# Reordering the split temporaries, the weight sums and the first stores in the seven-product units of an attention-and-mixer kernel

## The chip, the cores and the metric

The kernel runs on one core of one Trainium2 chip. The metric is the device time of one execution in microseconds. Five engines matter here: PE (TensorE: matmul, with its weight loads, PEld, shown apart), DVE (VectorE), ACT (ScalarE), POOL (GpSimd), and SP (SyncE), whose queue issues nearly all DMAs. Each engine works through its own queue in the order in which the program gives it instructions; engines wait for one another through semaphores.

## The reference

The kernel computes two things in a row. The first is a decayed linear attention over blocks of 64 rows; its output x has 4 batches of 768 x 512. The second is a mixer over it, and this is where the change lies:

```python
xt = x.transpose(0, 2, 1)
h = np.maximum(xt @ w_tok1, 0.0) @ w_tok2          # token mixing, 768 -> 256 -> 768
u = x + h.transpose(0, 2, 1)
h2 = np.maximum(u @ w_ch1, 0.0) @ w_ch2            # channel mixing, 512 -> 1536 -> 512
return (u + h2).astype(np.float32)
```

All is in float32. A matrix product is made of three matmuls of halved operands: each operand is split into a high part (a rounded copy, made by ACT) and a low part (source minus high part, made by POOL or DVE), and the products high-high, low-high and high-low are summed in PSUM.

## The kernel before

**Units.** Channel mixing is cut into 24 units. A unit is one pair (g, b): a group g of 256 of the 1536 hidden channels (six groups, 0 to 5) for a batch b. Units 0 to 11 run through the groups upwards for batches 0 and 1; units 12 to 23 run through them downwards for batches 2 and 3, with units 21 and 22 swapped, so 21 is (0, 2) and 22 is (1, 3). The names in the code: `NP1` = 12, `FIRST` = 14, `NU` = 24.

**Seven products in place of eight.** Both matrix products of a unit are done on blocks of 2 x 2 with seven block products in place of eight. The first, u @ w_ch1, takes the hidden products m1 to m7 (six matmuls of 128 x 384 each). Its operands are blocks of u and differences of blocks (B11, B21, B22, T1 to T4), and combinations of weight blocks.

In most units the second product, hidden @ w_ch2, takes plain blocks: four pairs (`out_pair`, twelve matmuls each). In the units of `SEVEN`, which are 14 to 20 and 22, it too takes seven products, M1 to M7 (`out_seven`, six matmuls each). For these the unit has to make from its hidden blocks h11, h12, h21 and h22 the differences T1 to T4, each with a high and a low part, and from the weights w_ch2 the same combinations, here called weight sums (`sum_steps`). A unit's second product is always worked through one unit later: while m1 to m7 of unit n run on PE, the pairs or M1 to M7 of unit n-1 run between them.

**What sets the order.** All is written out by hand: the engines take their instructions in the order of the program. `SLOTS_OF` (L1106) lists for each kind of unit the order of hidden products (m), output products (M) or pairs (numbers 0 to 3), and of the step t. `background(n)` lists work put between the slots, each with the place from which it may go: a product counts 6 places and a pair 12 (`T_M`, `T_P`), a step such as t none, and after each slot all work whose place has been reached is issued.

**The steps of a seven-product unit** (`mixing_seven`, L866):

- m1: ACT copies the bank to scratch a (L890). m2: DVE adds (L895), ACT takes the relu (L896): this is h11, and its parts are made (`parts_of`: cast on ACT, L884; subtraction on POOL, L885).
- m6: builds on m1's bank; ACT copies it to scratch b (L901). m5: a copy to scratch c (L906). m7: builds on m1's bank, DVE adds (L910), relu (L911): h22 in c, and its parts. m3: builds on m5's bank, DVE adds (L916), relu (L917): h12 in b.
- t: a = b - a is T1 (L920), and its parts; b = c - b is T3 (L922); c = c - a is T2 (L923), and its parts.
- m4: builds on m1's bank; ACT takes the relu to scratch d (L928): h21. Then the parts of h21 and those of T3.
- The fourth difference, d - c (L934), and its parts are put behind m1 of the next unit (`fourth`).

The parts of T1 to T4 lie in one tile, `late_t`.

**Output products.** M1, M6, M7 and M4 use one PSUM pair, `pa` of L980, and M5, M3 and M2 another, `pc`; there are two pairs of banks in all. Behind each product DVE adds the pair to the result in `uT` (L986; for the plain pairs L1021), and a later product on the same pair waits for that addition. M5 is the first to use its pair, so it waits for the addition that last read those banks in the unit before: M4's, or that of the last plain pair.

**Weight sums.** `load_sums(g)` (L946) loads the saved w_ch2 group from DRAM by one DMA into a raw tile; `sum_steps(g)` gives eight steps: two splits (cast on ACT, L374; subtraction on POOL, L375), four DVE combinations (L548 to L551), and two more splits. They must be done before the output products of group g start.

**Stores.** A finished quarter of a batch is turned by two DVE transposes (L1040) into one of two buffers, `hh0` and `hl0`, in turn, and goes out by eight DMAs on SP (L1046). There are eight such stores for batches 0 and 1, called store 0 to 7 here. The raw weight groups from the second on use the buffer `hh0` too; the first (group 4) takes batch 0's `uT0`. SP also issues the loads that bring back saved weights (`restore`, L1093).

Of the kernel before, what the change touches and what calls it, by code (L numbers as in the profile page):

```python
# [22 lines left out]
def kernel(  # L23
# [171 lines left out]
    n = 1  # L195
# [201 lines left out]
    def words(b):  # L397
        return uT[b].rearrange("p t s -> p (t s)").bitcast(U32)
# [245 lines left out]
    for i in range(-2, NI):  # L644
# [26 lines left out]
        n = early.get(i, len(work) // 4)  # L671
# [28 lines left out]
        if i == 5:  # L700
            weights[0] = group_tiles(0, False)
            w, w3 = words(2), words(3)
# [12 lines left out]
        if i == 10:  # L715
            homes[0] = {"B11": (up, None, 1), "B21": (up, None, 1), "T2": (kp, "kn", 2), "T1": (kp, "qn", 2)}
            homes[0] |= {"B22": (kp, "kr", 2), "T3": (kp, "kT", 2), "T4": (kp, "qT", 2)}
            first = build(0, 0, on_vector=("T1", "T2", "T3", "T4", "B22"))
# [38 lines left out]
    steps = {}  # L757
# [15 lines left out]
    NP1 = NG * 2  # L773
    FIRST = NP1 + 2
    units = [(g, b) for g in range(NG) for b in (0, 1)] + [(g, b) for g in reversed(range(NG)) for b in (2, 3)]
    units[-3], units[-2] = units[-2], units[-3]
    NU = len(units)
    SEVEN = [n for n in range(FIRST, NU - 1) if units[n][0] > 0]
    hs = {}
    scratch, fourth = {}, {}  # L780
    late = {}

    def take_scratch():
# [83 lines left out]
    def mixing_seven(n):  # L867

        key = units[n]
        hs[n] = {}  # L870
        at = {}
        a, b, c, d = (scratch[x] for x in (f"a{n % 2}", f"b{n % 2}", "c", "d"))
        vec = nc.vector

        def parts_of(o, src):
            if o[0] == "T":
                if "T" not in late:
                    late["T"] = upool.tile([P, 8, SB], F32R, tag="uT0", name="late_t")
                k = 2 * int(o[1]) - 2
                hh, hl = late["T"][:, k], late["T"][:, k + 1]  # L880
            else:
                hh, hl = (cp.tile([P, SB], F32R, tag=f"h{o}{x}" + "0" * (o != "11"), name=f"h{o}{x}{n}") for x in "hl")
            hs[n][o] = hh, hl
            nc.scalar.copy(out=hh, in_=src)  # L884
            nc.gpsimd.tensor_sub(out=hl, in0=src, in1=hh.bitcast(F32))  # L885

        def m1():
            at["a"] = bank("xT" if n % 2 else "sh", f"pa{n}", SB)
            prod(key, at["a"], A11, "B11", True)
            nc.scalar.copy(out=a, in_=at["a"])  # L890

        def m2():
            at["b"] = bank("sh", f"pb{n}", SB)
            prod(key, at["b"], A12, "B21", True)
            vec.tensor_add(out=a, in0=at["b"], in1=a)  # L895
            nc.scalar.activation(a, a, AF.Relu)  # L896
            parts_of("11", a)

        def m6():
            prod(key, at["a"], S2, "T2", False)  # L900
            nc.scalar.copy(out=b, in_=at["a"])  # L901

        def m5():
            at["c"] = bank("sh", f"pc{n}", SB)
            prod(key, at["c"], S1, "T1", True)
            nc.scalar.copy(out=c, in_=at["c"])  # L906

        def m7():
            prod(key, at["a"], S3, "T3", False)
            vec.tensor_add(out=c, in0=at["a"], in1=c)  # L910
            nc.scalar.activation(c, c, AF.Relu)  # L911
            parts_of("22", c)

        def m3():
            prod(key, at["c"], S4, "B22", False)
            vec.tensor_add(out=b, in0=at["c"], in1=b)  # L916
            nc.scalar.activation(b, b, AF.Relu)  # L917

        def t():
            vec.tensor_sub(out=a, in0=b, in1=a)  # L920
            parts_of("T1", a)
            vec.tensor_sub(out=b, in0=c, in1=b)  # L922
            vec.tensor_sub(out=c, in0=c, in1=a)  # L923
            parts_of("T2", c)

        def m4():
            prod(key, at["a"], A22, "T4", False)
            nc.scalar.activation(d, at["a"], AF.Relu)  # L928
            parts_of("21", d)
            parts_of("T3", b)  # L930

        def u():
            e = cp.tile([P, SB], F32, tag="h12h0", name=f"t4_{n}")
            vec.tensor_sub(out=e, in0=d, in1=c)  # L934
            parts_of("T4", e)

        fourth[n] = u

        return {"m1": m1, "m2": m2, "m3": m3, "m4": m4, "m5": m5, "m6": m6, "m7": m7, "t": t}

    sums_of = {}

    def load_sums(g):
        pool, tag = (upool, "uT0") if g == NG - 2 else (hidp, "hh0")
        late["raw", g] = pool.tile([P, JG * DM], U32, tag=tag, name=f"sums_raw{g}")
        nc.sync.dma_start(out=sum_raw(g), in_=saved_c2[g])  # L946

    def sum_raw(g):
        return late["raw", g]

    def sum_steps(g):
        low = c2_tile(f"s{g}", g % 2).rearrange("p a t j -> p (a t j)")[:, 0 : NW * 2 * P]
        low = low.rearrange("p (m t j) -> p m t j", t=2, j=P)
        if g % 2:
            if "odd" not in late:
                late["odd"] = upool.tile([P, NW, 2, P], F32R, tag="uT1", name="sums_odd")
            high = [late["odd"][:, x] for x in range(NW)]
        else:
            h0, h1 = (cp.tile([P, 4, 2, P], F32R, tag=f"cs{x}", name=f"sums{g}{x}") for x in range(2))
            high = [(h0, h1)[x // 4][:, x % 4] for x in range(NW)]  # L960
        sums_of[g] = high, low
        v = [x.bitcast(F32).rearrange("p (m t j) -> p m t j", t=2, m=2) for x in (sum_raw(g)[:, 0:DM], sum_raw(g)[:, DM:])]
        if g % 2:
            return split_seven(high[A11], low[:, A11], [late["odd"][:, x : x + 2] for x in (0, 2, 4)], low, v, nc.vector)
        return split_seven(high[A11], low[:, A11], [h0[:, 0:2], h0[:, 2:4], h1[:, 0:2]], low, v, nc.vector)
# [61 lines left out]
    def store(b, x, between=None):  # L1027

        sh, t = x // 2, 2 * (x % 2)
        k = 2 * b + sh  # L1030
        y = ytags[0]
        ytags.rotate(-1)
        if isinstance(y, str):
            y = hidp.tile([P, 1024], F32, tag=y, name=f"y{k}{t}")
        y = y[:, : 2 * SB]
        y = y.rearrange("p (blk t q) -> p blk t q", t=2, q=32)
        ub = uT[b][:, t : t + 2, sh * SB : (sh + 1) * SB]
        to = out[b, sh * SB : (sh + 1) * SB].rearrange("(blk s) (t q c) -> q s blk t c", s=32, t=4, q=4)
        for tt in (t, t + 1):
            nc.vector.transpose(out=y[:, :, tt - t, :], in_=ub[:, tt - t])  # L1040
            if between and tt == t:
                between()
        for m in range(4):
            for tt in (t, t + 1):
                eng = nc.scalar if k == LAST - 1 and tt == 3 and m >= 2 else nc.sync
                eng.dma_start(out=to[m, :, :, tt], in_=y[m * 32 : (m + 1) * 32, :, tt - t])  # L1046
# [48 lines left out]
    def temp_tiles():  # L1095
# [9 lines left out]

    SLOTS_OF = {  # L1106
        (False, False): ("m1", "m6", 0, 1, "m2", "m7", "m5", 2, "m4", 3, "m3"),
        (True, False): ("m1", 0, 1, "m2", "m6", "m5", 2, "m7", "m3", "t", 3, "m4"),
        (True, True): "m1 M1 m2 M5 m6 M6 m5 M3 m7 M7 m3 M2 t m4 M4".split(),
        (False, True): "m1 M1 m6 M5 m2 M6 m7 M3 m5 M7 m4 M2 m3 M4".split(),  # L1110
    }

    def background(n):

        g, b = units[n]
        ev = []

        def add(when, *fs):
            ev.extend((when, f) for f in fs)
# [82 lines left out]
        if n == NP1 + 1:  # L1202
# [1 line left out]
            add(6, bl["T4.h"])  # L1204
            add(12, bl["T4.l"])
            add(36, bl["B22"])
        if n == NP1:
            add(84, lambda: store(0, 0))
            add(90, lambda: store(0, 1))
        if n == NP1 + 1:  # L1210
            add(36, lambda: store(0, 2))
            add(60, lambda: store(0, 3), lambda: load_sums(g - 1))
        if n == FIRST:
            add(24, lambda: store(1, 0))
            add(66, lambda: store(1, 1))
        if n == FIRST + 1:
            add(12, lambda: store(1, 2))
            add(48, lambda: store(1, 3))
        if FIRST < n < NU - 4 and n % 2:
            add(72, lambda: load_sums(g - 1))  # L1220
        if n in SEVEN and n % 2 == 0 and g not in sums_of:
            ss = sum_steps(g)
            add(12, ss[0], ss[1])
            add(48, *ss[2:7])
            add(60, ss[7])
        if n >= NU - 2:
            x = 2 * (n - NU + 2)
            add(36, lambda: store(2, x))
            add(84, lambda: store(2, x + 1))
# [9 lines left out]
    def run(n, slots):  # L1239
        ev, at, ms = background(n), 0, (mixing_seven if n in SEVEN else mixing)(n)  # L1240
        if n - 1 in SEVEN:
            ms |= out_seven(n - 1)
            ms["m1"] = lambda first=ms["m1"]: [first(), fourth[n - 1]()]
        for x in slots:
            if isinstance(x, str):
                ms[x]()
                at += T_M if len(x) > 1 else 0
            else:
                out_pair(x[0], x[1])
                at += T_P  # L1250
            while ev and ev[0][0] <= at:
                ev.popleft()[1]()
        while ev:
            ev.popleft()[1]()
# [53 lines left out]
```

## Time and profile before

| | |
|---|---|
| median of 3 runs | 569.49 us (569.33 to 569.65) |
| profiled execution | 569.2 us, of which the span 567.3 us |
| granted PE clock in it | 0.995 |
| PE, PEld busy | 545.4 us (96%), 528.2 us (93%) |
| DVE, ACT, POOL busy | 445.8 us (79%), 244.2 us (43%), 276.6 us (49%) |
| moved by DMA | 65.72 MB, a mean of 116 GB/s |

The span runs from the first to the last instruction of the program; some 1.9 us of the execution's time lie around it. In the rows, times are from the start of the span. A timeline row gives start, duration, engine, line of the kernel, operation, what is written and read, shape and count, and in brackets the engine's idle time before it and who ended it. A row of waits gives who waited for whom, the total in us, how many times, and the longest. Matmuls overlap: the next starts before the one before has ended.

### The profile page before, as it was taken

The page shows a single profiled execution, that of the slowest core. Times are in us where ns is not written, and L with a number is a line of the kernel's source. Part 1 is how long each engine was busy: PE and PEld are TensorE (multiplying, and loading weights), DVE is VectorE, ACT ScalarE, POOL GpSimd, SP SyncE. Part 2 cuts the span into 40 slices and gives each one's busy share as a digit, 9 for nine tenths or more (in the row PEclk, how much of TensorE's full clock was granted, in tenths as well). Part 3 has the DMA queues.
Part 4 walks back from the last instruction along what each step waited for, and adds up shares of the span by engine and source line. Part 5 has one row for each costly group of instructions (what it writes and reads, how often), then busy time and mean ns, then how long its engine had stood idle before and what let it go on. Part 6 is the DMA issues. An engine that isn't in the chain of part 4 may idle for free.

```text
span 567.3 us, 10786 instructions
## 1 busy us (share of the span) xinstructions
PE 545.4 (96%) x4186; PEld 528.2 (93%) x4186; DVE 445.8 (79%) x650; ACT 244.2 (43%) x490; POOL 276.6 (49%) x248
## 2 busy tenths in 40 slices
PE   5998999999999999999999999999989999999994
PEld 4887898999999999999999999999989999999994
DVE  4788887787786989788778787797588878886783
ACT  3465432435263454443434444444344455442421
POOL 6666642737214563534444444643456767572330
PEclk9999999999999999999999999999999999999998
DMA  9999999998003523442617200005846131320237
GB/s 185 256 230 199 180 180 195 197 170 150 1 3 112 200 80 130 143 153 74 242 39 241 75 0 1 1 3 87 213 69 188 55 113 56 112 75 1 34 58 133
DMA packets 176020, 65.72 MB, mean 116 GB/s; under 512 B 163553, under 2 KB 166753, under 8 KB 175969
## 3 DMA queue, kind: packets, MB, share of 16 engines
q1 hardware_dynamic: 172224, 63.75, 47.6%
q10 hardware_dynamic: 3744, 1.28, 0.9%
q8 instruction: 33, 0.54, 0.4%
q14 instruction: 19, 0.15, 0.1%
HBM read 48.24 MB, written 16.78 MB: 115 GB/s over the span
## 4 chain that ended last, share of the span: by engine, by line
PE 77%; DVE 11%; DMA 5%; ACT 2%; SPq 2%; issue 2%; ACTq 0%; DVEq 0%
PE po L1006 21%; PE pa L795 9%; PE pc L795 8%; PE pb L795 6%; PE ph L451 6%; PE pa L980 4%; PE pc L980 4%; PE pd L795 3%; PE pu L488 3%; PE xT L323 2%; PE sc L299 2%; DMA qn<-in_q_dram 2%; PE xT L333 2%; PE pu L471 1%; DMA c1lr<-dc1l 1%
## 5 line engine op out<-in xcount | busy, mean ns | idle before, releaser
L1021 DVE TENSOR_TENSOR uT<-po,uT 128x768 f32<-128x768 f32 x62 | 59.0, 953 | 23.8 <-PE po L1006 23.6
L286 POOL COPY stb<-sv 64x320 f32<-64x320 f32 x32 | 26.8, 839 | 43.4 <-DVE sv L273 42.5
L806 ACT ACTIVATE c<-c 128x384 f32<-128x384 f32 x42 | 22.1, 526 | 59.6 <-DVE c L851 32.5
L340 ACT COPY uT<-xT 128x384 f32<-128x384 f32 x32 | 15.3, 477 | 48.5 <-PE xT L333 48.5
L323 PE MATMUL xT<-a,vn 128*64 128x128 f32 x384 | 35.5, 277 | 0.0
L986 DVE TENSOR_TENSOR uT<-pa,uT 128x768 f32<-128x768 f32 x32 | 30.4, 948 | 5.6 <-PE pa L980 5.6
L808 POOL TENSOR_TENSOR h22l<-c,h22h 128x384 fp32r<-128x384 f32 x14 | 14.4, 1029 | 40.1 <-ACT h22h L807 40.1
L307 DVE TENSOR_TENSOR a<-sc,mask 128x768 f32<-128x768 f32 x32 | 29.1, 949 | 5.9 <-PE sc L299 5.7
L333 PE MATMUL xT<-qs,stb 128*64 128x128 f32 x320 | 31.1, 273 | 0.0
L375 POOL TENSOR_TENSOR c1l<-cs,c1h 128x512 fp32r<-128x512 f32 x15 | 19.2, 1292 | 23.2 <-ACT c1h L374 23.2
L986 DVE TENSOR_TENSOR uT<-pc,uT 128x768 f32<-128x768 f32 x24 | 22.8, 949 | 9.3 <-PE pc L980 9.3
L451 PE MATMUL ph<-xhi,w1h 128*128 128x256 f32 x96 | 28.2, 294 | 0.8 <-DVE uT L493 0.5
L1006 PE MATMUL po<-h12h,c 128*128 128x384 f32 x112 | 28.7, 337 | 0.0
L1006 PE MATMUL po<-h11h,c 128*128 128x384 f32 x112 | 28.6, 336 | 0.0
L1006 PE MATMUL po<-h22h,c 128*128 128x384 f32 x112 | 28.6, 336 | 0.0
L1006 PE MATMUL po<-h21h,c 128*128 128x384 f32 x112 | 28.6, 336 | 0.0
L451 PE MATMUL ph<-xhi,w1l 128*128 128x256 f32 x96 | 27.1, 282 | 0.0
L451 PE MATMUL ph<-xlo,w1h 128*128 128x256 f32 x96 | 27.1, 282 | 0.0
L299 PE MATMUL sc<-qT,kT 64*128 64x128 f32 x384 | 26.0, 282 | 0.2 <-ACT qT L237 0.2
L299 PEld LDWEIGHTS sc<-qT,kT 64*128 64x128 f32 x384 | 22.9, 189 | 3.3 <-issue 1.8
L252 POOL TENSOR_TENSOR qs<-qT,lamp 128x640 f32<-128x640 f32 x16 | 25.3, 1583 | 0.3
L364 DVE TENSOR_TENSOR xlo<-xp,xhi 128x384 fp32r<-128x384 f32 x32 | 17.7, 552 | 9.1 <-ACT xhi L363 8.8
(402 smaller groups left out, 1947.5 us busy)
## 6 DMA issues: line engine op xcount, KB each, us to landing
raw<-in_moe_w_ch_dram SPq DMA_DIRECT2D x20, 512.0 KB, 3.8
vn<-in_v_dram SPq DMA_DIRECT2D x16, 384.0 KB, 5.3
kn<-in_k_dram SPq DMA_DIRECT2D x30, 192.0 KB, 5.0
out_dram<-y SPq DMA_DIRECT2D x96, 48.0 KB, 1.9
qn<-in_q_dram SPq DMA_DIRECT2D x44, 96.0 KB, 3.4
kr<-in_k_dram SPq DMA_DIRECT2D x32, 96.0 KB, 3.4
dc1h<-c1h SPq DMA_DIRECT2D x4, 768.0 KB, 5.3
dc1l<-c1l SPq DMA_DIRECT2D x4, 768.0 KB, 6.7
```

What stands on the lines that cost most here:

```text
L252: nc.gpsimd.tensor_mul(out=qss[i], in0=qTs[i][:, P:].rearrange("p (c i) -> p c i", i=P), in1=lamp[:, p, None, :].broadcast_to([P, NC - 1, P]),
L286: nc.gpsimd.tensor_copy(out=st[r, :, h, :], in_=sv[r].rearrange("p (e c) -> p c e", c=NC - 1))
L299: nc.tensor.matmul(out=sc[h][:, c * P : (c + 1) * P], lhsT=kTs[i][r, cs], rhs=qTs[i][r, cs], start=True, stop=True,)
L307: nc.vector.tensor_mul(out=a, in0=pair.rearrange("p h (c i) -> p h c i", i=P), in1=mask[:, 2 * p : 2 * p + 2, None, :].broadcast_to([P, 2, ...
L323: nc.tensor.matmul(out=xT[h * D : (h + 1) * D, cs], lhsT=vns[i][:, h, c, :], rhs=weights_of[i, g, h][:, cg, :], start=(cg == 0), stop=False,)
L333: nc.tensor.matmul(out=xT[h * D : (h + 1) * D, cs], lhsT=st[:, c - 1, h, :], rhs=qss[i][:, c - 1, :], start=False, stop=(cg == 2),)
L451: nc.tensor.matmul(out=ph, lhsT=w[:, c, fs], rhs=x[:, c], start=(i == 0), stop=(i == 3 * NC - 1))
L795: nc.tensor.matmul(out=to, lhsT=w[:, t], rhs=x[:, t], start=(start and i == 0), stop=(i == 5), skip_group_check=not start,)
L980: nc.tensor.matmul(out=pair[x][:, t], lhsT=w[:, t], rhs=h, start=(start and i == 0), stop=(i == 2), skip_group_check=not start,)
L986: nc.vector.tensor_add(out=ub, in0=pair[x], in1=ub)
L1006: nc.tensor.matmul(out=to, lhsT=w[:, jj, t * P : (t + 1) * P], rhs=h, start=(i == 0), stop=(i == 3 * JG - 1))
L1021: nc.vector.tensor_add(out=ub, in0=po, in1=ub)
```

## The change

No operation on data is added or removed; five things are moved.

- The subtraction that makes T2 and T2's parts leave step t and become a step w of its own, issued after m4 (and after M4 or the last pair).
- The parts of h21 and of T3 leave m4 and go to the step behind m1 of the next unit, ahead of T4's parts.
- The weight sums of groups 3, 2 and 1 are spread over two units: two steps in the odd unit before (place 48), the others in the even one (places 36 and 42). Those of group 4 stay within unit 14, the first two from place 6 in place of 12.
- The loads of the raw groups move: group 4 from place 60 to 36 of unit 13; groups 3, 2 and 1 from place 72 of units 15, 17 and 19 to place 84 of units 14, 16 and 18.
- The eight first stores, at 84 and 90 of unit 12, 36 and 60 of unit 13, 24 and 66 of unit 14, and 12 and 48 of unit 15, go to 36 and 72 of unit 12, 12, 36 and 66 of unit 13, and 12, 36 and 91 of unit 14 (91 is the end of the unit).

```diff
             vec.tensor_sub(out=b, in0=c, in1=b)
+
+        def w():
             vec.tensor_sub(out=c, in0=c, in1=a)
             parts_of("T2", c)
 
         def m4():
             prod(key, at["a"], A22, "T4", False)
             nc.scalar.activation(d, at["a"], AF.Relu)
-            parts_of("21", d)
-            parts_of("T3", b)
 
         def u():
             e = cp.tile([P, SB], F32, tag="h12h0", name=f"t4_{n}")
             vec.tensor_sub(out=e, in0=d, in1=c)
+            parts_of("21", d)
+            parts_of("T3", b)
             parts_of("T4", e)
 
-        fourth[n] = u
+        rest[n] = u
...
-        (True, False): ("m1", 0, 1, "m2", "m6", "m5", 2, "m7", "m3", "t", 3, "m4"),
-        (True, True): "m1 M1 m2 M5 m6 M6 m5 M3 m7 M7 m3 M2 t m4 M4".split(),
+        (True, False): ("m1", 0, 1, "m2", "m6", "m5", 2, "m7", "m3", "t", 3, "m4", "w"),
+        (True, True): "m1 M1 m2 M5 m6 M6 m5 M3 m7 M7 m3 M2 t m4 M4 w".split(),
...
-        if n == NP1:
-            add(84, lambda: store(0, 0))
-            add(90, lambda: store(0, 1))
+        first, times = {NP1: (0, (36, 72)), NP1 + 1: (2, (12, 36, 66)), FIRST: (5, (12, 36, 91))}.get(n, (0, ()))
+        for x, when in enumerate(times, first):
+            add(when, lambda x=x: store(x // 4, x % 4))
         if n == NP1 + 1:
-            add(36, lambda: store(0, 2))
-            add(60, lambda: store(0, 3), lambda: load_sums(g - 1))
+            add(36, lambda: load_sums(g - 1))
         if n == FIRST:
-            add(24, lambda: store(1, 0))
-            add(66, lambda: store(1, 1))
-        if n == FIRST + 1:
-            add(12, lambda: store(1, 2))
-            add(48, lambda: store(1, 3))
-        if FIRST < n < NU - 4 and n % 2:
-            add(72, lambda: load_sums(g - 1))
-        if n in SEVEN and n % 2 == 0 and g not in sums_of:
             ss = sum_steps(g)
-            add(12, ss[0], ss[1])
+            add(6, ss[0], ss[1])
             add(48, *ss[2:7])
             add(60, ss[7])
+        if FIRST <= n < NU - 5 and n % 2 == 0:
+            add(84, lambda: load_sums(g - 1))
+        if FIRST < n <= NU - 4:
+            if n % 2:
+                late["steps"] = ss = sum_steps(g - 1)
+                add(48, ss[0], ss[1])
+            else:
+                ss = late["steps"]
+                add(36, *ss[2:7])
+                add(42, ss[7])
...
-            ms["m1"] = lambda first=ms["m1"]: [first(), fourth[n - 1]()]
+            ms["m1"] = lambda first=ms["m1"]: [first(), rest[n - 1]()]
```

More of the change, by code (lines that the diff above doesn't have):

```diff
@@ L779 @@
     hs = {}
-    scratch, fourth = {}, {}
+    scratch, rest = {}, {}
     late = {}
@@ L934, in u @@
             vec.tensor_sub(out=e, in0=d, in1=c)
+            parts_of("21", d)
+            parts_of("T3", b)
             parts_of("T4", e)
-        fourth[n] = u
-        return {"m1": m1, "m2": m2, "m3": m3, "m4": m4, "m5": m5, "m6": m6, "m7": m7, "t": t}
+        rest[n] = u
+        return {"m1": m1, "m2": m2, "m3": m3, "m4": m4, "m5": m5, "m6": m6, "m7": m7, "t": t, "w": w}
     sums_of = {}
```

## The prediction

> **What bounds the kernel now.** I read the page's engine shares first, then TensorE's (PE's) own waits, then the starts of the units in the timeline, and last the engines around each loss.
>
> ```profile
> PE 545.4 (96%) x4186; PEld 528.2 (93%) x4186; DVE 445.8 (79%) x650; ACT 244.2 (43%) x490; POOL 276.6 (49%) x248
> ```
>
> PE is busy for 96% of the span, and the diff changes no matmul. So the change can win only stalls of PE, and lose only by making new ones. PE's waits, as waiting instruction, releaser, total us, times and longest; the one that touches the change's units most:
>
> ```profile
> PE pc L980 <- ACT scratch_d L928: 2.3, 4, 1.4
> ```
>
> The same view cut to the late units adds PE's weight loads, and one idle time of POOL that I need below:
>
> ```profile
> POOL h22l L885 <- ACT h22h L884: 16.0, 4, 4.3
> ...
> PEld pa L795 <- ACT scratch_a L890: 1.0, 3, 0.3
> ```
>
> The view's other long waits are on loads at the start and out of the change's reach. What these cost is read from the first matmul of each unit (product m1 of units 14 to 23):
>
> ```profile
> 394.99 0.34 PE L795 MATMUL pa<-B11h,a11h 128*128 128x384 f32 x1
> 411.51 0.33 PE L795 MATMUL pa<-B11h,a11h 128*128 128x384 f32 x1
> 428.18 0.34 PE L795 MATMUL pa<-B11h,a11hr 128*128 128x384 f32 x1
> 442.87 0.34 PE L795 MATMUL pa<-B11h,a11hr 128*128 128x384 f32 x1
> 458.42 0.35 PE L795 MATMUL pa<-B11h,a11hr 128*128 128x384 f32 x1
> 473.13 0.33 PE L795 MATMUL pa<-B11h,a11hr 128*128 128x384 f32 x1
> 488.70 0.34 PE L795 MATMUL pa<-B11h,a11hr 128*128 128x384 f32 x1
> 503.39 0.35 PE L795 MATMUL pa<-B11h,a11hr 128*128 128x384 f32 x1
> 518.91 0.34 PE L795 MATMUL pa<-B11h,a11hr 128*128 128x384 f32 x1
> 534.78 0.34 PE L795 MATMUL pa<-B11h,a11hr 128*128 128x384 f32 x1
> ```
>
> Units 15 to 21 have 84 matmuls each. Units 16, 18 and 20 take 14.69, 14.71 and 14.69 us, which is 0.175 us a matmul and 1.05 us a product of six. Unit 15 takes 16.67, 17 takes 15.55, 19 takes 15.57 and 21 takes 15.52: they lose 1.98, 0.86, 0.88 and 0.83. Units 14 and 22 have the same slots; they take 16.52 and 15.87, so unit 14 loses 0.65. Together 5.20 us. That is more than the waits add up to, since products right behind a wait are stretched too.
>
> **T2 behind the read of M4: 4.55 us.** Unit 17, the pattern of 19 and 21:
>
> ```profile
> 442.64 1.53 DVE L922 TENSOR_TENSOR scratch_b<-scratch_c,scratch_b 128x384 f32<-128x384 f32 x1
> 444.28 1.19 DVE L923 TENSOR_TENSOR scratch_c<-scratch_c,scratch_a 128x384 f32<-128x384 f32 x1
> 445.39 0.94 DVE L986 TENSOR_TENSOR uT<-pa,uT 128x768 f32<-128x768 f32 x1
> ...
> 442.11 1.65 POOL L375 TENSOR_TENSOR c2s<-sums_raw,sums_odd 128x512 fp32r<-128x512 f32 x1
> 443.72 1.32 POOL L885 TENSOR_TENSOR late_t<-scratch_a,late_t 128x384 fp32r<-128x384 f32 x1
> ...
> 442.64 0.51 ACT L884 CAST late_t<-scratch_a 128x384 fp32r<-128x384 f32 x1 [0.69 <-DVE scratch_a L920]
> 445.50 0.51 ACT L884 CAST late_t<-scratch_c 128x384 fp32r<-128x384 f32 x1 [2.34 <-DVE scratch_c L923]
> 445.91 0.48 ACT L928 ACTIVATE scratch_d<-pa 128x384 f32<-128x384 f32 x1
> ...
> 447.26 0.47 ACT L890 COPY scratch_a<-pa 128x384 f32<-128x384 f32 x1
> ...
> 445.84 0.34 PE L795 MATMUL pb<-B21l,c1hr 128*128 128x384 f32 x1
> 446.48 0.41 PE L980 MATMUL pc<-late_t,sums_odd 128*128 128x384 f32 x1 [0.29 <-ACT scratch_d L928]
> 447.79 0.44 PE L795 MATMUL pa<-T2h,c1hr 128*128 128x384 f32 x1
> ```
>
> M5 starts at 446.48 where it could at 446.02 (445.84 and 0.175). In the code it opens a new PSUM pair, and that pair's bank was last read by the sum of M4 (L986, done 446.33); the relu of d (L928, done 446.39) ends 0.06 later, so the trace can't part them. It needn't: both stand behind T2. L986 is queued on DVE behind T2's subtraction (L923), and the relu on ACT behind T2's cast (445.50), which waited 2.34 us for it. The change puts both first. L986 then starts at L922's end, 444.17, and is done at 445.1; the relu follows T1's cast (443.15) and is done at 443.6. M5 has 0.9 us to spare. For unit 15:
>
> ```profile
> 413.80 1.41 DVE L923 TENSOR_TENSOR scratch_c<-scratch_c,scratch_a 128x384 f32<-128x384 f32 x1
> 415.13 0.94 DVE L1021 TENSOR_TENSOR uT<-po,uT 128x768 f32<-128x768 f32 x1
> ...
> 416.23 0.41 PE L980 MATMUL pc<-late_t,sums 128*128 128x384 f32 x1 [1.41 <-ACT scratch_d L928]
> ```
>
> Here the sum of the last pair (L1021) holds the bank. Without the 1.33 us from L923 to it, it ends at 414.74, some 0.1 after m2 (411.51 and three products); and DVE comes to this place earlier too, since unit 14 loses its own delay (below). I take all 1.98.
>
> What is late next is m6, which builds on the bank that L890 copies. Two casts (21 and T3, a step of 0.42 each) leave the ACT queue ahead of L890. With L923 at 445.1 and done by 445.7, T2's cast ends at 446.2 and L890 at 446.6; m6 is due at 442.87 + 4 x 1.05 = 447.07. That is 0.4 us to spare, in the worst unit as it was before. If L923 kept its 1.19 there, m6 would lose 0.2 us in each of three units: the upper bound of this part's residue is 0.6.
>
> L923's length is a question of its own. In these rows L922 took 1.53 us and ended 0.41 after POOL's c2s (443.76), and L923 ended 0.43 after POOL's T1 (445.04). [...]
>
> **21 and T3 a unit on.** Their casts and POOL subtractions now start behind L890, with T4's. POOL does T2, 21, T3 and T4 in 1.0 to 1.3 us each and is through by about 6.5 us into the unit; M7 reads T3 at 9.45 and M2 reads 21 at 11.55. Cost nothing, 3 us of cover; without it, each late us would count in every unit.
>
> **Weight sums over two units.** No operation is added. The first two (casts, and 2 us of POOL) go to the odd unit's M3, in front of L911; POOL's idle of up to 4.3 us ahead of h22l (row above) hides them, and without it they would delay c in the odd unit. The rest moves up to M6 in the even unit, and there ACT's copy of c (L906) is now queued behind a cast that waits for L550:
>
> ```profile
> 434.67 0.96 DVE L986 TENSOR_TENSOR uT<-pa,uT 128x768 f32<-128x768 f32 x1 [0.67 <-PE pa L980]
> ...
> 439.00 0.62 ACT L374 CAST sums_odd<-sums_raw 128x512 fp32r<-128x512 f32 x1 [2.76 <-DVE sums_raw L550]
> ...
> 438.67 0.34 PE L795 MATMUL pc<-B22h,c1hr 128*128 128x384 f32 x1
> ```
>
> From M6's sum (ends 435.63) three subtractions of 0.45 bring L550 to 437.0; cast to 437.6, L906 to 438.0; m3 builds on that bank at 438.67. Estimate: 0.6 us to spare, cost 0. If DVE were 1 us later, 0.4 in each of units 16, 18, 20: 1.2 us.
>
> **First stores and the load of unit 14's sums: 0.65 us.**
>
> ```profile
> 381.62 17.86 SPq L1046 DMA_DIRECT2D out_dram<-y  x32
> 399.52 0.48 SPq L946 DMA_DIRECT2D sums_raw<-dc  x1
> ...
> 403.81 0.41 ACT L374 CAST sums<-sums_raw 128x256 fp32r<-128x256 f32 x1 [6.57 <-DMA sums_raw<-dc]
> 405.61 0.47 ACT L901 COPY scratch_b<-pa 128x384 f32<-128x384 f32 x1
> 406.13 0.44 PE L795 MATMUL pa<-T3h,c1h 128*128 128x384 f32 x1 [0.53 <-ACT scratch_b L901]
> ```
>
> The load is issued behind 32 store DMAs (0.56 us each); ACT's casts wait for it, L901 for them, m7 for L901. An 0.7 us earlier load is enough. After, only stores 2 and 3 stand near it: 16 DMAs from about 385.5, where unit 13's DVE queue has come past T4's low part by its slots (an estimate, as are the store times below). It is issued at about 394.5, 5 us earlier.
>
> The stores use two buffers, and DVE, which fills them, waits with its whole queue when one isn't drained:
>
> ```profile
> 387.70 1.04 DVE L1040 STREAM_TRANSPOSE y<-uT 128x384 f32<-128x384 f32 x2 [0.27 <-DMA out_dram<-y]
> 402.00 8.82 SPq L1046 DMA_DIRECT2D out_dram<-y  x8
> 394.57 1.03 POOL L808 TENSOR_TENSOR h21l<-c,h21h 128x384 fp32r<-128x384 f32 x1 [2.06 <-ACT h21h L807]
> ```
>
> A buffer is free 6.1 us after its first DMA (381.62 to 387.70, where store 2 waited for store 0), or some 11 us when it stands behind the restored weights (8.82 for eight DMAs, and 2 to land). Store 4 falls behind unit 13's third pair, about 391.8, when store 2's buffer is just free (its first DMA about 385.5, and 6.1: 391.6); it puts h21l some 0.6 us later than 394.57, due at about 396.9. Store 7 is filled behind T2 of unit 14, about 412, and waits for store 5, issued from about 400.4 behind the restored weights: free at about 411. Behind it stand L934 (to 414.0, held up by one POOL operation) and M1's sum, to 415.0; M6 of unit 15 needs that at 410.86 + 5.25 = 416.1. One us each, so 0 here; both ends: 0 to 2.5.
>
> **The sum.** 4.55 + 0.65 = 5.20 us off the profiled execution: its span of 567.3 goes to 562.1, and with the 1.9 us around it 569.2 goes to 564.0. The median of the runs is 0.29 above that execution, so 564.3.
>
> **The rivals.**
> 1. *The wait only moves on.* m6 on L890, or m3 on L906 (0.2 to 0.4 us in three units each, priced above): 0.6 to 1.8 back, about 565.5. For it: margins of 0.4 to 0.6. Against: unit 16's lighter sums pull DVE and POOL forward.
> 2. *A store's buffer is late.* Up to 2.5 us back in units 14 and 15, about 566.3. [...] Against: the rows leave a us at both places.
> 3. *DVE is locked out by the gathered POOL work, slower than before.* T2, 21, T3 and T4 now run back to back on POOL at each unit's start, just where DVE's fourth difference (L934, two SBUF inputs) stands in front of M1's sum, on which M6 builds. M1's sum should end 3.15 us into a unit, M6 starts at 5.25, and one shut-out costs 1.0 to 1.3. It counts from the second in a row, and beyond 0.75 us in each of 7 units the kernel is slower than before. Three in a row are 3.45 us, less the 2.1 to spare: 1.35 a unit, 9.5 in all, 573.8. Against: L934 starts at about 2 us in, with at most one POOL operation ahead. [...]
> 4. *It doesn't do what it says:* M5's wait hangs on something I don't see in its semaphores; only unit 14's 0.65 is won: 568.8.
>
> **Chances.** Forecast 0.64 (its own range 563.9 to 564.9), rival 1 0.16, rival 2 0.12, rival 3 0.04, rival 4 0.04. The range goes from 563.9 to 566.6, which takes in rivals 1 and 2. A measurement tells about 0.2% (1.1 us) from no change. Rival 4 straddles that bound, and I add mixtures of 1 to 3: faster 0.91, same 0.04, slower 0.05.
>
> **What would show it.** Units 15, 17, 19, 21 of 14.7 us, and unit 14 of 15.9; no wait of M5 on L928; ACT's first sum cast of unit 14 without its 6.57 us; the relu L928 ahead of T2's cast. A wait of PE on L890, L906 or a sum L986, or of DVE on out_dram, would name rival 1, 3 or 2. I am wrong if the odd units keep 15.5 us, or if an even one grows.

## The result and the profile after

| | before | after |
|---|---|---|
| median, first comparison (5 runs each) | 569.65 us | 565.76 us (563.98 to 567.26) |
| ratio, 95% interval | | 0.9931 (0.9913 to 0.9948) |
| median, second comparison (17 and 6 runs) | 569.77 us (568.49 to 572.70) | 564.72 us (563.72 to 568.12) |
| ratio, 95% interval | | 0.9909 (0.9881 to 0.9938) |
| profiled execution: time, span | 569.2, 567.3 us | 563.98, 562.1 us |

The kernel is faster by 0.7 to 0.9%. In the second comparison the medians are 5.05 us apart. The page of the changed kernel, its span and PE's share:

```profile
span 562.1 us, 10783 instructions
PE 543.0 (97%) x4186; PEld 528.5 (94%) x4186; DVE 435.2 (77%) x650; ACT 244.4 (43%) x490; POOL 272.4 (48%) x248
```

In the changed kernel some lines have other numbers (L980 is L982, L986 is L988, L1021 is L1023, L923 is L925, L928 is L930, L946 is L948, L1040 is L1042). The view of PE's waits, cut to 392 to 520 us (units 14 to 22), is empty: there is a head and no row under it.

```profile
core 0 of [0], span 562.1 us
engine line waited for: us in total, times, longest us
```

The first matmul of product m1 of units 14 to 23, from the changed kernel's timeline (start, duration):

```profile
395.09 0.34 PE L795 MATMUL pa<-B11h,a11h 128*128 128x384 f32 x1
410.75 0.33 PE L795 MATMUL pa<-B11h,a11h 128*128 128x384 f32 x1
425.47 0.34 PE L795 MATMUL pa<-B11h,a11hr 128*128 128x384 f32 x1
440.16 0.34 PE L795 MATMUL pa<-B11h,a11hr 128*128 128x384 f32 x1
454.90 0.35 PE L795 MATMUL pa<-B11h,a11hr 128*128 128x384 f32 x1
469.62 0.33 PE L795 MATMUL pa<-B11h,a11hr 128*128 128x384 f32 x1
484.33 0.34 PE L795 MATMUL pa<-B11h,a11hr 128*128 128x384 f32 x1
499.03 0.35 PE L795 MATMUL pa<-B11h,a11hr 128*128 128x384 f32 x1
513.74 0.34 PE L795 MATMUL pa<-B11h,a11hr 128*128 128x384 f32 x1
529.61 0.34 PE L795 MATMUL pa<-B11h,a11hr 128*128 128x384 f32 x1
```

Unit 14 takes 15.66 us and units 15 to 21 take 14.69 to 14.74 each: every odd unit is as short as the even ones to 0.05 us. From the start of unit 14 to that of unit 23 there were 139.79 us before and are 134.52 now. That is 5.27 us, and the spans differ by 5.2, so all of the gain lies here.

Unit 17 in the timeline, by engine (DVE, ACT, PE), to be held against the rows of unit 17 in the prediction:

```profile
439.71 0.56 DVE L922 TENSOR_TENSOR scratch_b<-scratch_c,scratch_b 128x384 f32<-128x384 f32 x1
440.36 0.96 DVE L988 TENSOR_TENSOR uT<-pa,uT 128x768 f32<-128x768 f32 x1
441.24 0.55 DVE L925 TENSOR_TENSOR scratch_c<-scratch_c,scratch_a 128x384 f32<-128x384 f32 x1
...
439.71 0.52 ACT L884 CAST late_t<-scratch_a 128x384 fp32r<-128x384 f32 x1 [1.39 <-DVE scratch_a L920]
440.13 0.49 ACT L930 ACTIVATE scratch_d<-pa 128x384 f32<-128x384 f32 x1
441.82 0.51 ACT L884 CAST late_t<-scratch_c 128x384 fp32r<-128x384 f32 x1 [1.20 <-DVE scratch_c L925]
442.24 0.47 ACT L890 COPY scratch_a<-pa 128x384 f32<-128x384 f32 x1
...
443.31 0.34 PE L982 MATMUL pc<-late_t,sums_odd 128*128 128x384 f32 x1
444.38 0.34 PE L795 MATMUL pa<-T2h,c1hr 128*128 128x384 f32 x1
```

M4's sum is now L988 and T2's subtraction L925. M4's sum ends at 441.32, 2.0 us ahead of M5, and the copy L890 ends at 442.71, 1.67 us ahead of m6 (444.38). L922, which took 1.53 us, takes 0.56; T2's subtraction takes 0.55 in place of 1.19.

The head of unit 14 (SP's queue, then ACT):

```profile
395.03 0.48 SPq L948 DMA_DIRECT2D sums_raw<-dc  x1
...
399.28 0.93 ACT L374 CAST sums<-sums_raw 128x256 fp32r<-128x256 f32 x2 [1.96 <-DMA sums_raw<-dc]
...
403.21 0.47 ACT L901 COPY scratch_b<-pa 128x384 f32<-128x384 f32 x1
```

The load is issued as unit 14 starts (395.09), where in the kernel before it was issued 4.5 us into the unit. ACT still waits for it, but in its own idle time, and L901 is done 8.6 us into the unit, well ahead of m7 (405.54, 10.45 us in).

### The profile page after: what moved, and what is told of

The parts are those of the page before. It is cut to its first block, busy times and chain, and to the rows that moved or that the text cites. A ratio compares the mean times of both kernels' runs of the same rounds, so it can differ in the third digit from the quotient of the medians.

```text
span 562.1 us, 10783 instructions
## 1 busy us (share of the span) xinstructions
PE 543.0 (97%) x4186; PEld 528.5 (94%) x4186; DVE 435.2 (77%) x650; ACT 244.4 (43%) x490; POOL 272.4 (48%) x248
## 4 chain that ended last, share of the span: by engine, by line
PE 86%; DVE 6%; DMA 3%; ACT 2%; SPq 1%; issue 1%; ACTq 0%; DVEq 0%
PE po L1008 23%; PE pa L795 12%; PE pc L795 9%; PE pb L795 7%; PE pa L982 6%; PE ph L451 6%; PE pc L982 5%; PE pd L795 3%; PE xT L323 3%; PE sc L299 2%; PE pu L488 2%; PE xT L333 2%; DMA kn<-in_k_dram 2%; PE pu L471 1%; DMA qn<-in_q_dram 1%; DVE xlo L364 1%
## 5 line engine op out<-in xcount | busy, mean ns | idle before, releaser
L1023 DVE TENSOR_TENSOR uT<-po,uT 128x768 f32<-128x768 f32 x62 | 59.0, 953 | 22.5 <-PE po L1008 22.2
L988 DVE TENSOR_TENSOR uT<-pa,uT 128x768 f32<-128x768 f32 x32 | 30.6, 957 | 11.0 <-PE pa L982 10.3
L988 DVE TENSOR_TENSOR uT<-pc,uT 128x768 f32<-128x768 f32 x24 | 22.9, 956 | 10.6 <-PE pc L982 10.6
```

The lines of the kernel that those rows point to most:

```text
L988: nc.vector.tensor_add(out=ub, in0=pair[x], in1=ub)
L1023: nc.vector.tensor_add(out=ub, in0=po, in1=ub)
```

## The experiments

The table gives unit lengths in us, worked out in each profiled execution from the starts of m1; each can be off by 0.01. Units 16, 18 and 20 are 14.69 to 14.72 in all of them but for one value, given with experiment 3, and unit 22 is 15.87. The last column is the sum of units 14 to 22.

| kernel | 14 | 15 | 17 | 19 | 21 | sum |
|---|---|---|---|---|---|---|
| before | 16.52 | 16.67 | 15.55 | 15.57 | 15.52 | 139.79 |
| the change | 15.66 | 14.72 | 14.74 | 14.71 | 14.71 | 134.52 |
| 2: order alone | 16.62 | 15.36 | 14.74 | 14.72 | 14.72 | 136.12 |
| 3: sums and stores alone | 15.67 | 14.89 | 14.74 | 14.72 | 14.72 | 135.19 |
| 4: stores and first load alone | 15.66 | 14.90 | 15.56 | 15.56 | 15.53 | 137.17 |
| 5: T2 alone | 15.67 | 16.01 | 15.08 | 15.09 | 15.05 | 136.87 |
| 6: parts of h21, T3 alone | 15.66 | 16.37 | 15.26 | 15.26 | 15.24 | 137.76 |
| 7: parts of h21, T3, T2 alone | 16.01 | 16.46 | 15.26 | 15.26 | 15.23 | 138.20 |
| 8: order and stores | 15.66 | 14.72 | 14.74 | 14.72 | 14.72 | 134.52 |

Experiments 5, 6 and 7 were timed once each (569.47, 567.62 and 568.36 us, beside a median of 569.17 for the kernel before), so they are read by their unit lengths alone.

**1. The changed kernel again.** There is no edit here; it was timed anew, since its first five runs were spread over 3.3 us.

> The changed kernel itself, timed again. The profile taken of it has no wait of PE left in units 14 to 22 and a span of 562.1 us, yet its runs lie between 563.98 and 567.26 us. Theory A (the spread is the granted clock: executions with a clock of 0.993 or 0.994 in place of 0.997 are longer by that share alone): the unit lengths at full clock stay 14.7 us, and each run's span follows its clock; ratio to before 0.991 at like clocks. Theory B (stalls come back in some executions): a longer run of the same clock, with units over 14.7 us.

Median 564.72 us, ratio 0.9909 (0.9881 to 0.9938). The unit lengths of this profile repeat those of the first to 0.01 us. But both traces are from the lower end of the times (563.98 and 564.44 us, of 563.72 to 568.12), so they don't show theory B wrong. Theory A fits in part. Of the eleven timings of the changed kernel, the five with a granted clock of 0.995 or more have spans of 561.7 to 562.8 us, the six with 0.994 or less 563.0 to 566.3. The order is the clock's. The size isn't: from 0.998 to 0.993 is 2.8 us of 562, and the spans differ by 4.6. Other profiles show where some of it may come from. Unit 0 (the first hidden product of channel mixing) starts at 182.5 us in this profile and the first one; in the profiles of the other experiments it starts at 182.4 to 185.6. From there to the start of unit 23 only units 14 to 21 differ, and what follows takes 32.4 to 32.9 us. The latest start is that of experiment 5. The windows around 55 us of the two kernels (length, then PE, PEld, DVE, ACT and POOL busy with counts, granted clock, DMA share, GB/s), first of experiment 5:

```profile
53.30:56.70 3.40, 3.40 (x19) 3.40 (x18) 1.49 (x2) 0.85 (x3) 0.51 (x1) 0.51 0.83 126
```

and of the changed kernel:

```profile
53.30:56.70 3.40, 3.40 (x37) 3.23 (x37) 1.35 (x4) 2.70 (x7) 2.51 (x2) 1.00 0.71 109
```

In experiment 5 PE worked for 3.4 us at half its clock and did 19 matmuls in place of 37. Such a stretch, always 3.4 us long and between 47 and 57 us, is in the profiles of experiments 2, 4, 5 and 8 and in none of the others. It comes behind a wait of PE of some 2 us there. Where there is no such stretch, unit 0 starts at 182.4 to 182.7, and once, in experiment 3, at 183.5; where there is one, at 183.3 to 185.6. So the opening of the kernel, which the change doesn't touch, spreads single executions over some 3 us. That it explains each of the longer times isn't shown, since each kernel has one trace, the changed one two.

**2. The order alone.** T2 behind the read of M4 and the parts of h21 and T3 a unit on; sums, loads and stores as before.

```diff
+        def w():
             vec.tensor_sub(out=c, in0=c, in1=a)
             parts_of("T2", c)
...
-            parts_of("21", d)
-            parts_of("T3", b)
...
             vec.tensor_sub(out=e, in0=d, in1=c)
+            parts_of("21", d)
+            parts_of("T3", b)
...
-... m3 M2 t m4 M4".split(),
+... m3 M2 t m4 M4 w".split(),
```

> Only the order of the seven-product steps is changed: T2 behind the read of M4, the parts of h21 and T3 a unit on. Weight sums, loads and first stores stay as before. The prediction's split: 4.55 us of the 5.20 come from here, so units 15, 17, 19, 21 take about 14.7 and unit 14 keeps 16.5; span about 562.8. Rival (the weight sums crowd DVE and POOL, and the order matters little): units 17, 19, 21 still take over 15.2, span over 564.5.

Median 566.24 us, ratio 0.9931 (0.9907 to 0.9954). Units 17, 19 and 21 come to full length by the order alone, as the prediction's split has it; unit 14 keeps its loss, and unit 15 keeps 0.64. PE's waits, cut to the late units:

```profile
PE pa L795 <- ACT scratch_b L901: 0.7, 1, 0.7
PE pa L795 <- ACT scratch_a L890: 0.2, 1, 0.2
```

The first is m7 of unit 14 behind the late load; the second is m6 of unit 15, on a copy that comes late because DVE's queue comes late out of unit 14 (experiment 4). So the 1.98 us of unit 15 are not the order's alone.

**3. The sums and stores alone.** The background work as in the changed kernel, the steps as before.

```diff
-        if n == NP1:
-            add(84, lambda: store(0, 0))
...
+        first, times = {NP1: (0, (36, 72)), NP1 + 1: (2, (12, 36, 66)), FIRST: (5, (12, 36, 91))}.get(n, (0, ()))
...
+                late["steps"] = ss = sum_steps(g - 1)
+                add(48, ss[0], ss[1])
```

> Only the weight sums, their loads and the first stores are moved; T2 stays ahead of the read of M4, the parts of h21 and T3 stay where they were. The prediction's split: only unit 14's 0.65 us, span about 566.7, M5 waits in 15, 17, 19, 21. Rival (overlap: the old order loses only where sums hold DVE up): with POOL's second sum gone from the place where it held L922 up for 1 us, M4's sum ends 1 us earlier than 446.33, M5 has 0.4 us to spare, and units 15, 17, 19, 21 come near 14.7 by this half alone: span near 562.3.

Median 565.28 us, ratio 0.9913 (0.9891 to 0.9935). The prediction's split is wrong here by 4 us: this half alone brings units 17, 19 and 21 to full length, with T2 still ahead of M4's sum. Its DVE rows of unit 17, and M5:

```profile
441.41 0.56 DVE L922 TENSOR_TENSOR scratch_b<-scratch_c,scratch_b 128x384 f32<-128x384 f32 x1
442.07 1.35 DVE L923 TENSOR_TENSOR scratch_c<-scratch_c,scratch_a 128x384 f32<-128x384 f32 x1
443.34 0.95 DVE L986 TENSOR_TENSOR uT<-pa,uT 128x768 f32<-128x768 f32 x1
...
445.01 0.34 PE L980 MATMUL pc<-late_t,sums_odd 128*128 128x384 f32 x1
```

L922 takes 0.56 us in place of 1.53, and M4's sum, still behind T2, ends at 444.29, 0.7 us ahead of M5. The half leaves 0.2 us in unit 15, and unit 16 takes 15.18 us, the one even unit that grew. The ACT queue of unit 15 in this kernel:

```profile
423.02 0.93 ACT L374 CAST sums_odd<-sums_raw 128x256 fp32r<-128x256 f32 x2 [2.97 <-DMA sums_raw<-dc]
423.86 0.52 ACT L911 ACTIVATE scratch_c<-scratch_c 128x384 f32<-128x384 f32 x1
```

ACT stands for 2.97 us before the load of group 3's weights has landed, and the relu of c waits behind it; all that follows is late, to M5 and m6 of unit 16. The whole change has the same wait (2.0 us in its unit 15) and loses nothing by it.

**4. The first stores and the load of group 4 alone.**

```diff
...
+        first, times = {NP1: (0, (36, 72)), NP1 + 1: (2, (12, 36, 66)), FIRST: (5, (12, 36, 91))}.get(n, (0, ()))
+        for x, when in enumerate(times, first):
+            add(when, lambda x=x: store(x // 4, x % 4))
         if n == NP1 + 1:
-            add(36, lambda: store(0, 2))
-            add(60, lambda: store(0, 3), lambda: load_sums(g - 1))
+            add(36, lambda: load_sums(g - 1))
...
```

> Only the eight first stores and the load of group 4's raw weights are moved. The prediction's split: unit 14's 0.65 us, span about 566.7, unit 15 still 16.7. Rival (unit 15's 1.98 us is mostly the lateness that unit 14 hands on): unit 15 comes to 14.7 to 15.2 too, span near 564.7; units 17, 19, 21 keep 15.5 by both.

Median 567.75 us, ratio 0.9955 (0.9939 to 0.9972). The rival holds: unit 15 comes from 16.67 to 14.90 without any change of order, so 1.77 of its 1.98 us was lateness out of unit 14. It is lateness of DVE's queue and not of unit 14's own length: in experiment 6, below, PE is through unit 14 in 15.66 us, and unit 15 still takes 16.37. The last pair's sum, for which M5 of unit 15 waits, in experiment 6 and in this one:

```profile
414.28 0.94 DVE L1021 TENSOR_TENSOR uT<-po,uT 128x768 f32<-128x768 f32 x1
...
413.00 0.94 DVE L1021 TENSOR_TENSOR uT<-po,uT 128x768 f32<-128x768 f32 x1
```

It starts 3.6 us into unit 15 there, as in the kernel before, and 1.3 here. The first combination of the weight sums (L548), which stands behind the load, starts 10.4 us into unit 14 there and 8.0 here; and there the transposes of a store (1.02 us) stand between L910 and L916. No run parts the stores from the load. The wait of M5 stays in units 17, 19 and 21:

```profile
PE pc L980 <- ACT scratch_d L928: 0.9, 3, 0.3
```

**5. T2 alone.** As 2, without the move of the parts of h21 and T3.

```diff
+        def w():
             vec.tensor_sub(out=c, in0=c, in1=a)
             parts_of("T2", c)
...
-... m3 M2 t m4 M4".split(),
+... m3 M2 t m4 M4 w".split(),
```

> From the kernel before, only T2 (subtraction and parts) is put behind the read of M4; the parts of h21 and T3 stay behind m4, so POOL and ACT now do them ahead of T2's. The prediction called their move free and M5's wait the larger part: units 17, 19, 21 then take 14.7 to 14.9, unit 15 about 15.4, unit 14 16.5; sum of units 14 to 22 about 136.3. Rival (the parts ahead of T2 make it late: POOL's subtraction for h21 shuts out DVE's T2, and T2's cast and ACT's copy of a behind it hold m6 up): a wait of PE on L890, units 17, 19, 21 at 15.0 to 15.4, the sum over 137.

Neither expectation names the main wait that came. Units 17, 19 and 21 stand at 15.05 to 15.09: M5 is on time in these units, but the next output product, M6, isn't. The waits of PE's weight loads in the late units, and POOL's queue around the start of unit 17:

```profile
PEld pa L982 <- POOL late_t L885: 1.9, 4, 0.7
```

```profile
446.71 1.36 POOL L885 TENSOR_TENSOR h21l<-scratch_d,h21h 128x384 fp32r<-128x384 f32 x1
448.04 1.33 POOL L885 TENSOR_TENSOR late_t<-scratch_b,late_t 128x384 fp32r<-128x384 f32 x1
449.32 1.02 POOL L885 TENSOR_TENSOR late_t<-scratch_c,late_t 128x384 fp32r<-128x384 f32 x1
```

The third row is T2's low part, which M6 reads. It stands behind the low parts of h21 and T3, which nobody needs for another 4 us. So the move of the parts isn't a side dish: without it the move of T2 gives back some 0.35 us in each of units 17, 19 and 21, and 0.65 in unit 15 (16.01 against 15.36 in experiment 2).

**6. The parts of h21 and T3 alone.** As 2, with T2 left in step t.

```diff
-            parts_of("21", d)
-            parts_of("T3", b)
...
             vec.tensor_sub(out=e, in0=d, in1=c)
+            parts_of("21", d)
+            parts_of("T3", b)
```

> From the kernel before, only the parts of h21 and T3 go behind m1 of the next unit; T2 stays ahead of the read of M4. By the prediction's reading M5's wait stays as it was (M4's sum is still behind T2) and only m6's wait on the copy of a goes, 0.1 to 0.2 us in units 15, 17, 19, 21: sum of units 14 to 22 about 139.2 against 139.8. Rival (POOL and ACT freed ahead of T2 bring M5 forward too): a sum under 138.5.

In units 15, 17, 19 and 21 it gains 1.2 us, 0.3 in each, where 0.1 to 0.2 was expected: m6 doesn't wait any more, and M5 waits as before.

```profile
PE pc L980 <- ACT scratch_d L928: 2.2, 4, 1.4
```

The rest of its smaller sum, which lies below the 138.5 set for the rival, comes from unit 14, whose code it doesn't touch: 15.66 us. SP's and ACT's rows show why:

```profile
398.89 0.48 SPq L946 DMA_DIRECT2D sums_raw<-dc  x1
...
402.94 0.93 ACT L374 CAST sums<-sums_raw 128x256 fp32r<-128x256 f32 x2 [5.67 <-DMA sums_raw<-dc]
404.74 0.47 ACT L901 COPY scratch_b<-pa 128x384 f32<-128x384 f32 x1
```

Unit 14 starts here at 395.03. The load is issued 3.86 us into it, against 4.53 in the profile before, and L901 is done at 10.2 us, just in time for m7. Over the five profiles with the old stores the load came 3.8 to 5.0 us into the unit, and unit 14 took 15.66 to 16.62. So the loss of unit 14 differs from execution to execution; with the stores moved, the load comes between 0.5 us ahead of the unit's start and 0.3 behind it in all five.

**7. The parts of T2, h21 and T3, with T2's subtraction left in its place.** This tells apart the two that M5 may wait for. Beside the edit of experiment 6:

```diff
             vec.tensor_sub(out=c, in0=c, in1=a)
+
+        def w():
             parts_of("T2", c)
```

> As in e6, and T2's parts (cast and POOL subtraction) go behind the read of M4, while DVE's T2 subtraction itself stays ahead of it. So the relu of d no longer stands behind T2's cast on ACT, and M4's sum still stands behind T2 on DVE. If M5 waits for the bank that M4's sum reads: M5's wait stays, units 17, 19, 21 at 15.3 to 15.5, sum about 139. If M5 waits for the relu of d, as the view of waits names it: the wait goes, units 17, 19, 21 at 14.7, sum about 136.5.

M5's wait stays. Unit 17 by engine (DVE, ACT, PE):

```profile
443.83 1.19 DVE L923 TENSOR_TENSOR scratch_c<-scratch_c,scratch_a 128x384 f32<-128x384 f32 x1
444.94 0.94 DVE L988 TENSOR_TENSOR uT<-pa,uT 128x768 f32<-128x768 f32 x1
...
442.61 0.49 ACT L930 ACTIVATE scratch_d<-pa 128x384 f32<-128x384 f32 x1
...
446.03 0.41 PE L982 MATMUL pc<-late_t,sums_odd 128*128 128x384 f32 x1 [0.29 <-ACT scratch_a L890]
```

The relu of d is done at 443.10, nearly 3 us ahead of M5, and M5 still starts only behind M4's sum (445.88). So M5 waits for the bank, and the releaser that the view of waits named before (the relu, L928) was only ACT's latest event; here it names L890, which M5 needs as little.

**8. Order and stores, the sums left in one unit each.** The edit is against the changed kernel.

```diff
...
-        if n == FIRST:
+        if FIRST < n < NU - 4 and n % 2:
+            add(72, lambda: load_sums(g - 1))
+        if n in SEVEN and n % 2 == 0 and g not in sums_of:
             ss = sum_steps(g)
-            add(6, ss[0], ss[1])
+            add(12, ss[0], ss[1])
             add(48, *ss[2:7])
             add(60, ss[7])
-        if FIRST <= n < NU - 5 and n % 2 == 0:
-            add(84, lambda: load_sums(g - 1))
...
```

> The change without the spreading of the weight sums: new order of the steps, first stores and first load moved, sums of groups 3, 2 and 1 in one unit each as before. If the order alone already covers units 17, 19, 21 and the stores unit 14 and 15, as the runs of each alone say, the sum of units 14 to 22 is 134.5 as with the whole change, and the spreading is worth nothing beside the other two. If the crowded sums still hold DVE up: 17, 19, 21 over 14.8, the sum over 134.9.

Median 564.86 us beside 569.17 before, ratio 0.9928 (0.9909 to 0.9946), and unit for unit the lengths of the whole change. Beside the other two, the spreading of the sums is worth nothing.

## Why the prediction was right, and where it wasn't

**The sum was right.** 5.20 us were forecast off the profiled execution and 5.2 came off it: the span went to 562.1 and the execution to 563.98 us, where 562.1 and 564.0 were forecast. It was the sum of all the stalls in these units, and it holds whichever move takes which, so the match says nothing for the split. Its terms are a little off either way: unit 14 gave 0.86 us, not 0.65 (it came down to 15.66, below the 15.87 of unit 22 against which it was measured), and the odd units 4.43, not 4.55. That one execution met 562.1 to the tenth is luck as well, since the spans of the changed kernel run from 561.7 to 566.3 us. The medians (565.76, then 564.72) lie in the range, the first of them outside the forecast's own 563.9 to 564.9; they stand above the forecast of 564.3 because of its last step. The offset of 0.29 us between execution and median was taken from three runs 0.3 us apart, while the opening of the kernel spreads executions over some 3 us. The first median's offset was 1.8 us.

**The mechanism of M5 was right, and the doubt about it is settled.** The bank's reader M4's sum holds M5, not the relu (experiment 7).

**The split was wrong.** The step that failed is "T2 behind the read of M4: 4.55 us". It took the losses of units 15, 17, 19 and 21 for the order's, and only 0.65 for the rest. The losses have several causes in a row on DVE's queue, and more than one of the moves takes each away:

- Unit 15's 1.98 us: 1.77 go with the stores and the first load alone (experiment 4), 1.31 with the order alone (experiment 2).
- Units 17, 19 and 21: the order alone takes all, and so do the spread sums with the stores. The stores alone take none of it (experiment 4), so in experiment 3 it is the sums. My own rows held this: L922 took 1.53 us with POOL's second sum at work beside it (to 443.76). In experiment 3, where the sums are moved, it takes 0.56, and with that 1 us gone M4's sum behind T2 ends 0.7 us before M5 is due. I noted the rows and didn't work out the second way.
- The gains alone are 3.67 (order) and 4.60 (sums and stores), 8.27 together; both at once give 5.27. Without unit 14, whose loss varies by itself (experiment 6), they are 3.77 and 3.75, and 4.41 at once. The order adds 0.67 to the other half, and the spread sums add nothing to order and stores.

**"21 and T3 a unit on: cost nothing"** is right of the move by itself, but that was the wrong question. It was priced by its own deadlines (M7, M2), which are far off. Its worth lies in what it clears from the front of T2 (experiment 5: 0.35 us in each of three odd units, and 0.65 in unit 15) and, where T2 stays, from the front of the copy for m6 (experiment 6: 0.3 in each).

**"Cost 0" for the sums** is right. The copy of c that was to be queued behind a cast has its margin, in unit 16 (ACT, then PE's m3):

```profile
434.20 0.62 ACT L374 CAST sums_odd<-sums_raw 128x512 fp32r<-128x512 f32 x1 [2.81 <-DVE sums_raw L550]
434.73 0.47 ACT L906 COPY scratch_c<-pc 128x384 f32<-128x384 f32 x1
...
435.96 0.34 PE L795 MATMUL pc<-B22h,c1hr 128*128 128x384 f32 x1
```

It ends 0.76 us ahead of m3, with 0.6 forecast. What I gave nothing was the wait of the two casts in the odd unit for their load: 2.0 us, at no cost beside the new order, and 0.49 in unit 16 without it (experiment 3).

**Stores.** Neither buffer was late. Stores 4 and 7 and what stands behind store 7, from DVE's queue, and M6 of unit 15:

```profile
391.96 1.03 DVE L1042 STREAM_TRANSPOSE y<-uT 128x384 f32<-128x384 f32 x2
...
412.06 1.03 DVE L1042 STREAM_TRANSPOSE y<-uT 128x384 f32<-128x384 f32 x2
413.01 1.17 DVE L934 TENSOR_TENSOR t<-scratch_d,scratch_c 128x384 f32<-128x384 f32 x1
414.11 0.95 DVE L988 TENSOR_TENSOR uT<-pa,uT 128x768 f32<-128x768 f32 x1
...
416.00 0.34 PE L982 MATMUL pa<-late_t,sums 128*128 128x384 f32 x1
```

Store 7 started at 412.06 (412 forecast), the fourth difference took 1.17 us and ended 0.41 behind POOL's low part of T2 (412.76 to 413.77), so it was held up by one POOL operation as forecast, and M1's sum ended at 415.06 (415.0 forecast), 0.9 us ahead of M6. The load of group 4 was issued at 395.03 (394.5 forecast).

**The margins that were too small:** M5 has 2.0 us (0.9 forecast), m6 1.67 (0.4 forecast). They were worked out from the old times of DVE, which the other moves brought forward. The 0.6 us that m6's margin gives to T2's subtraction behind M4's sum is my estimate: no row of the kernel before shows it (the subtraction takes 1.18 to 1.41 there), and in unit 17 of the changed kernel it takes 0.55.

**The rivals.** The first (the wait moves on to L890 or L906), the second (a late buffer) and the third (DVE shut out by POOL) show nowhere in the changed kernel. Of the third, the fourth difference was held up once, to 1.17 us, in unit 15 above; in units 16 to 21 it takes 0.56 us. The fourth (it doesn't do what it says) fell.

## What to carry to other kernels

A stall at the end of a queue has a chain of causes, and each move that takes a microsecond out of the chain may end it alone; so gains of parts must not be added, and each part's worth is asked with the other parts in place. When work is put behind something, look at what then stands ahead of it: here the low parts that no one needed yet decided whether the move paid. Where a view of waits names a releaser that the code doesn't link to the waiting instruction, look for another engine's event just before it.

## What the runs showed of the hardware that was not expected

In four of ten profiles PE ran at half clock for one stretch of 3.4 us between 47 and 57 us (a granted clock of 0.51 in the window of experiment 5 above). Before it PE had waited 1.95 to 2.39 us at L265; in the six profiles without a stretch it waited 1.47 to 2.16 us there, so the length of this wait doesn't decide it alone. In experiment 5 a second wait followed, of 2.02 us on DVE, in the changed kernel one of 0.45. What sets off such a stretch, and what sets its length, no run here shows.

The other, which the prediction weighed, is the length of a DVE subtraction beside POOL's work. T2's subtraction in unit 17, the same instruction on the same operands, took 1.19 us where POOL was at work on T1 (443.72 to 445.04), and 0.55 behind M4's sum, where POOL's T1 ended (441.32) just as it began (441.24). Why it is longer beside POOL no run here shows.
